# Moving one transposed piece of v from TensorE to the DMA, and the loads behind it to new places

## The chip, the cores and the metric

The kernel runs on one core of one Trainium2 chip. The metric is the device time of one execution in microseconds (us), median of several runs. The kernel before takes 569.44 us (three runs, 569.25 to 569.69). A profile's "span" is about 1.75 us shorter than the time of the same run (567.7 for a run of 569.45 us), so spans are compared with spans.

Engine names: PE is TensorE, DVE VectorE, ACT ScalarE, POOL GpSimd, SP SyncE; PEld is the weight load of TensorE. "L157" is line 157 of a kernel; the changed kernels have a few lines more or less, so the same statement can carry another number.

## The reference, cut to what matters

```python
# q, k, v: (4, 5824, 256)
qn = q / (norm(q, axis=1) + 1e-6);  kn = k / (norm(k, axis=1) + 1e-6)
a = softmax(kn.T @ qn / tau)                 # 256 x 256 for each batch
x = (v @ a).reshape(23296, 256)
out = (((x @ w1) * (x @ w2)) @ w3) @ w_out   # d_ff = 1024
```

The kernel folds `a` into w1 and w2 (a matrix Wf for each batch) and w3 into w_out (W_sb, once). For each chunk of 512 tokens there are then eight units of two products a and b from v transposed (each two matmuls of 512 columns), a multiply of the two, and output matmuls with W_sb.

## The kernel before

v arrives in six pieces of 8 x 128 tokens for each batch (the last is shorter); chunks 2p and 2p+1 use piece p. v has to be transposed, on PE (with a copy out of PSUM) or by a DMA transpose from SP:

```python
def transpose_half_on_pe(n, pi, h, on_act): ...      # 8 PE transposes, one copy on ACT or DVE
def transpose_piece(n, pi):
    ...
    nc.sync.dma_start_transpose(vT[:, pi * PIECE : (pi + 1) * PIECE, :, :], t[:, :, :])
```

All loads are issued by GpSimd, in program order, but for the first half pieces of q and k. Two kinds of tiny copies hold that queue back: `gate` reads the newest product (so the queue does not run ahead of PE), `hold` reads one element of a tile that a transpose writes (so the queue stands until the transpose has landed):

```python
def gate():                      # waits for the newest a*b tile
    nc.gpsimd.tensor_copy(gate_t, last_ab[0][:1, :1])
def hold(src):                   # waits for whatever writes src
    nc.gpsimd.tensor_copy(gate_t, src)
```

An agenda says at which place of PE's own order ("clock", in estimated us of PE work) each piece of side work is emitted, `at(place, cost, what)`. For batch 0:

```python
load_piece("v", 0, 1); load_piece("v", 0, 2)
nc.gpsimd.dma_start(out=wout_sb, ...); nc.gpsimd.dma_start(out=w3_bf, ...)     # right behind v
...
at(7.0, 0.5, lambda: transpose_half_on_pe(0, 1, 0, True))
at(8.0, 0.5, lambda: transpose_half_on_pe(0, 1, 1, False))
at(15.0, 0.0, transpose_w3)                       # four DMA transposes
at(15.0, 0.0, lambda: transpose_piece(0, 2))
for jt in range(FT):                              # w3 into w_out, 64 matmuls
    at(27.5 + 1.2 * jt, 0.87, lambda jt=jt: w_unit(jt))
moves = [("qk", 1, 0, 29.0), ("v", 0, 3, 30.0), ("v", 0, 4, 30.5), ("qk", 1, 1, 44.0), ...]
```

Output matmuls may start only when the eight w units are done; until then PE runs a and b units. The G matmuls (q and k of the next batch) are spread over the middle of each batch.

Of the kernel before, what the change touches and what calls it, by code (L numbers as in the profile page):

```python
# [15 lines left out]
P = 128  # L16
PIECE = 8
# [8 lines left out]
def kernel(  # L26
# [12 lines left out]
    nc = tc.nc  # L39
# [11 lines left out]
    FT = F // P  # L51
# [3 lines left out]
    NP_ = (NT + PIECE - 1) // PIECE  # L55
# [59 lines left out]
    def load_piece(nm, n, pi, cuts=()):  # L115

        new_piece(nm, n, pi)
        ends = [0, *cuts, LAST if pi == NP_ - 1 else PIECE]
        for lo, hi in zip(ends, ends[1:]):
            load_part(nm, n, pi, lo, hi)  # L120

    vTs = {}

    def new_vT(n):
        vTs[n] = (
            vT_pool.tile([P, NT - 1, CT, P], BF16, tag="vT", name=f"vT_{n}"),
            vT_pool.tile([P, CT, P + LEFT], BF16, tag="vTt", name=f"vTt_{n}"),
        )

    def pe_transpose(dst, src, tag, on_act):  # L130

        m = psum.tile([P, 8, P], BF16, tag=tag, name=f"tr_{nc.get_next_instruction_name()}", bufs={"ab": 4, "out": 3}[tag])
        for i, blk in enumerate(src):
            nc.tensor.transpose(m[:, i, :], blk, ident_b)
        if on_act:
            nc.scalar.copy(dst, m)
        else:
            nc.vector.tensor_copy(dst, m)

    def transpose_half_on_pe(n, pi, h, on_act):  # L140
        if pi == 0 and h == 0:
            new_vT(n)
        t = pieces["v", n, pi]
        i0 = 4 * h
        pe_transpose(
            vTs[n][0][:, pi * PIECE + i0 : pi * PIECE + i0 + 4, :, :].rearrange("p i c t -> p (i c) t"),
            [t[:, i0 + i, ct * P : (ct + 1) * P] for i in range(4) for ct in range(CT)],
            "out", on_act,
        )

    def transpose_piece(n, pi):
        if pi == 0:
            new_vT(n)
        vT, vTt = vTs[n]
        t = pieces.pop(("v", n, pi))
        if pi < NP_ - 1:
            nc.sync.dma_start_transpose(vT[:, pi * PIECE : (pi + 1) * PIECE, :, :], t[:, :, :])  # L157
        else:
            g = LAST - 1
            nc.sync.dma_start_transpose(vT[:, pi * PIECE : pi * PIECE + g, :, :], t[:, :g, :])  # L160

            first = n % 2 == 0
            nc.sync.dma_start_transpose(vTt[:, :, :P] if first else vTt[:, :, LEFT:], t[:, g, :])
            nc.sync.dma_start_transpose(vTt[:, :, P:] if first else vTt[:, :, :LEFT], t[:LEFT, g + 1, :])
# [52 lines left out]
    def squares(nm, pi, slots, end=False):  # L217

        if nm not in S:
            S[nm] = psum.tile([P, CT, P], F32, tag="out", name=f"sq{nm}_0", bufs=3)  # L220
        t = pieces[nm, 0, pi]
        for i in slots:
            for ct in range(CT):
                cs = slice(ct * P, (ct + 1) * P)
                nc.tensor.matmul(  # L225
                    S[nm][:, ct, :], lhsT=t[:, i, cs], rhs=t[:, i, cs],
                    start=(pi == 0 and i == 0 and ct == 0),
                    stop=(end and i == slots[-1] and ct == CT - 1), skip_group_check=True,
                )
# [211 lines left out]
    def at(t, cost, fn):  # L441
        seq[0] += 1
        agenda.append((t, seq[0], cost, fn))
# [22 lines left out]
    def hold(src):  # L466

        nc.gpsimd.tensor_copy(gate_t, src)  # L468
# [81 lines left out]
    def load_qk(n, pi):  # L550
        load_piece("q", n, pi)
        load_piece("k", n, pi)
# [13 lines left out]
    w3_bf = w3_wout[:, : FT * F].rearrange("p (j l) -> p j l", l=F)  # L566
    wout_sb = w3_wout[:, FT * F : FT * (F + D)].rearrange("p (l d) -> p l d", d=D)
    w3T = []
# [20 lines left out]
    w3r = moe_w3.rearrange("(jh jl) l -> jl jh l", jl=P)  # L589
# [29 lines left out]
    load_part("v", 0, 0, half, PIECE)  # L619
    load_piece("v", 0, 1)  # L620
    load_piece("v", 0, 2)
    nc.gpsimd.dma_start(out=wout_sb, in_=moe_w_out.rearrange("(lh ll) c -> ll lh c", ll=P))
    nc.gpsimd.dma_start(out=w3_bf, in_=w3r)
    squares("k", 4, whole)
    for sl in (lo, hi):
        squares("q", 4, sl)
# [19 lines left out]
    def w_unit(jt):  # L646
        m = psum.tile([P, 512], F32, tag="out", name=f"w_{jt}", bufs=3)
        for lt in range(FT):
            nc.tensor.matmul(  # L649
                m[:, :D], lhsT=w3T[jt // 2][:, jt % 2, lt, :], rhs=wout_sb[:, lt, :],  # L650
                start=(lt == 0), stop=(lt == FT - 1),
            )
        if jt % 2 == 0:
            nc.scalar.copy(W_sb[:, jt, :], m[:, :D])
        else:
            nc.vector.tensor_copy(W_sb[:, jt, :], m[:, :D])
        if jt == FT - 1:
            w_ready[0] = True

    def load_library():  # L660

        m = work.tile([P, 1], F32, tag="lib", name="lib", bufs=1)
        nc.gpsimd.partition_all_reduce(m, ones_f, P, ReduceOp.add)


    def make_agenda(b):
        agenda.clear()
        clock[0] = 0.0
        n = b + 1
        if b == 0:  # L670
            at(0.5, 0.87, soft0[5])
            for i in range(4):
                at((1.7, 2.6, 3.5, 3.9)[i], 0.43, soft0[7 + i])
            at(0.0, 0.0, load_library)
            at(4.6, 0.5, lambda: transpose_half_on_pe(0, 0, 1, False))
            at(7.0, 0.5, lambda: transpose_half_on_pe(0, 1, 0, True))
            at(8.0, 0.5, lambda: transpose_half_on_pe(0, 1, 1, False))
            at(15.0, 0.0, transpose_w3)
            at(15.0, 0.0, lambda: transpose_piece(0, 2))
            for jt in range(FT):  # L680
                at(27.5 + 1.2 * jt, 0.87, lambda jt=jt: w_unit(jt))
            moves = [("qk", 1, 0, 29.0), ("v", 0, 3, 30.0), ("v", 0, 4, 30.5), ("qk", 1, 1, 44.0), ("qk", 1, 2, 45.0)]
            moves += [("qk", 1, 3, 53.0), ("qk", 1, 4, 55.0), ("v", 0, 5, 61.0), ("qk", 1, 5, 73.0)]
            moves += [("v", 1, 0, 88.0), ("v", 1, 1, 98.0), ("v", 1, 2, 120.0), ("qk", 2, 0, 130.0)]
            t0, t1 = 54.0, 113.0
        else:
            moves = [("v", b, 3, 1.0), ("qk", n, 1, 10.0), ("qk", n, 2, 17.0), ("v", b, 4, 26.0), ("qk", n, 3, 38.0)]
            moves += [("v", b, 5, 46.0), ("qk", n, 4, 58.0), ("qk", n, 5, 66.0)]
            moves += [("v", n, 0, 76.0), ("v", n, 1, 86.0), ("v", n, 2, 96.0), ("qk", n + 1, 0, 108.0)]
            moves = [m for m in moves if m[1] < B]  # L690
            t0, t1 = 16.0, 98.0

        before = (0, 2) if b == 0 else None
        for nm, m, pi, t in moves:
            if before is not None and not (nm == "v" and before == (m, pi - 1) == (0, 3)):
                at(t, 0.0, lambda w=before: hold(vTs[w[0]][1][:1, 0, :1] if w[1] == NP_ - 1 else vTs[w[0]][0][:1, w[1] * PIECE, 0, :1]))
            at(t, 0.0, gate)
            if nm == "qk":
                at(t, 0.0, lambda m=m, pi=pi: load_qk(m, pi))
                before = None  # L700
            else:
                at(t, 0.0, lambda m=m, pi=pi: load_piece("v", m, pi))
                at(t + 4.0, 0.0, lambda m=m, pi=pi: transpose_piece(m, pi))
                before = (m, pi)
        if n == B:
            agenda.sort()
            return
        units = score_units(n)
        for i, (cst, fn) in enumerate(units):
            at(t0 + (t1 - t0) * i / len(units), cst, fn)  # L710
        soft = soft_units(n)
        for cst, t, fn in soft:
            at(t1 + 1.0 + t, cst, fn)
        agenda.sort()

    for b in range(B):
        make_agenda(b)
        for c in range(NCH):
            for j in range(FT):
                run_due()  # L720
                emit_ab(b, c, j)
                npop = 0
                lag = LAG
                if b == B - 1 and c >= NCH - 2:
                    lag = LAG_END if c == NCH - 1 else LAG + (LAG_END - LAG) * (j + 1) // FT
                while w_ready[0] and len(pend) > lag and npop < 2:
                    emit_out(*pend.pop(0))
                    npop += 1
                    run_due()
        run_due(1e9)  # L730
# [39 lines left out]
```

## Time and profile before

| | kernel before |
|---|---|
| time, median | 569.44 us |
| span | 567.7 us |
| PE busy | 557.6 us (98%) |
| chain that ended last | PE 93%, DMA 5% |
| first a matmul | 37.27 us |
| PE's last group of output matmuls starts | 562.19 us |
| from there to the end of the span | 5.51 us |

A line of a timeline: start and length in us, engine, line, operation, how many.

```profile
562.19 1.47 PE L521 MATMUL o<-W_sb,left 128*128 128x256 bf16 x12
```

### The profile page before, as it was taken

The numbers are of one execution on the slowest core, as the hardware profiler recorded it, in microseconds if no ns is written. First come the engines' busy times: TensorE is split into PE (matmuls) and PEld (weight loads), VectorE is DVE, ScalarE is ACT, GpSimd is POOL, SyncE is SP. The second block draws the span as 40 slices with busy tenths as digits, with TensorE's granted clock in tenths as the row PEclk, the third lists the DMA queues.
The fourth block names the chain that finished last, engine by engine and source line by source line (L and its number), as shares of the span: only waits on it lengthen the run. The fifth ranks groups of instructions, "written<-read, shape, count | busy, mean of one in ns | idle before, by whom it ended". The sixth has DMA issues, their size and how long they took to land.

```text
span 567.7 us, 10095 instructions
## 1 busy us (share of the span) xinstructions
PE 557.6 (98%) x3755; PEld 355.4 (63%) x3755; DVE 375.4 (66%) x581; ACT 338.7 (60%) x627; POOL 77.9 (14%) x163
## 2 busy tenths in 40 slices
PE   8799999999999999999999999999999999999997
PEld 5664566776656666666656566666655655665655
DVE  1047645888966577888766668787876665565564
ACT  1057536777766577777675567777765554454453
POOL 4260013120111111121210101030120000000000
PEclk9999999999999999999999999999999999999999
DMA  9999989978455796595661595765740325221011
GB/s 213 211 182 209 173 171 237 226 164 192 115 142 121 143 192 148 90 193 123 145 149 75 97 219 117 155 120 121 185 112 39 85 74 149 64 68 71 38 70 61
DMA packets 75104, 77.45 MB, mean 136 GB/s; under 512 B 54192, under 2 KB 58800, under 8 KB 75056
## 3 DMA queue, kind: packets, MB, share of 16 engines
q0 software_dynamic: 15760, 38.93, 39.3%
q1 hardware_dynamic: 59008, 37.23, 22.0%
q10 hardware_dynamic: 288, 0.66, 0.4%
q8 instruction: 29, 0.48, 0.3%
q14 instruction: 19, 0.16, 0.1%
HBM read 78.91 MB, written 23.86 MB: 181 GB/s over the span
## 4 chain that ended last, share of the span: by engine, by line
PE 93%; DMA 5%; ACT 1%; POOL 0%; issue 0%; DVE 0%; ACTq 0%; POOLq 0%
PE o L521 28%; PE b L476 28%; PE a L476 28%; PE G L192 5%; DMA k<-in_k_dram 5%; PE fold L363 2%; PE w L649 1%; ACT kr L283 0%; PE quarter L389 0%; POOL k L111 0%; POOL q L111 0%; PE sqk L225 0%; PE row L271 0%; ACT e L322 0%; ACT Wf L398 0%
## 5 line engine op out<-in xcount | busy, mean ns | idle before, releaser
L497 DVE TENSOR_TENSOR abs<-as,b 128x512 bf16<-128x512 bf16 x336 | 230.6, 687 | 143.9 <-ACT as L482 131.4
L482 ACT CAST as<-a 128x512 bf16<-128x512 f32 (+1 forms) x384 | 215.9, 562 | 170.4 <-DVE abs L497 84.7
L476 PEld LDWEIGHTS <-Wf 128*128 128x128 bf16 x1536 | 149.0, 98 | 102.3 <-ACT Wf L398 0.6
L476 PE MATMUL a<-vT,Wf 128*128 128x512 bf16 x704 | 209.6, 379 | 0.4 <-ACT Wf L398 0.4
L476 PE MATMUL b<-vT,Wf 128*128 128x512 bf16 x704 | 209.6, 379 | 0.0
L521 PE MATMUL o<-W_sb,abs 128*128 128x256 bf16 x1344 | 201.5, 273 | 0.0
L521 PEld LDWEIGHTS <-abs 128*128 128x128 bf16 x1344 | 131.2, 98 | 79.8 <-issue 0.2
L201 DVE TENSOR_TENSOR acc<-acc,sq 128x1024 f32<-128x1024 f32 x66 | 80.4, 1219 | 0.6 <-ACT sq L189 0.6
L192 PE MATMUL G<-k,q 128*128 128x256 bf16 x276 | 49.8, 273 | 0.0
L189 ACT ACTIVATE sq<-q 128x512 f32<-128x512 bf16 x66 | 41.8, 633 | 0.0
L189 ACT ACTIVATE sq<-k 128x512 f32<-128x512 bf16 x66 | 41.5, 629 | 0.0
L464 POOL COPY gate_t<-abs 1x1 bf16<-1x1 bf16 x39 | 10.5, 269 | 171.7 <-DVE abs L497 168.8
L543 DVE COPY osb<-o 128x512 f32<-128x512 f32 x44 | 30.1, 685 | 0.9 <-PE o L521 0.9
L192 PEld LDWEIGHTS <-q 128*128 128x128 bf16 x276 | 27.0, 98 | 3.1
L542 ACT COPY osb<-o 128x512 f32<-128x512 f32 x44 | 25.8, 586 | 4.1 <-PE o L521 2.1
L468 POOL COPY gate_t<-vT 1x1 bf16<-1x1 bf16 x16 | 3.1, 193 | 158.8 <-DMA vT<-v 158.8
L111 POOL DMA_DIRECT2D q<-in_q_dram x28 | 15.1, 540 | 12.5 <-DMA k<-in_k_dram 5.5
L370 ACT ACTIVATE Wf<-fold,rs 128x512 bf16<-128x512 f32 x15 | 10.3, 687 | 10.9 <-PE fold L363 8.7
L283 ACT ACTIVATE kr<-row 128x256 f32<-128x256 f32 x1 | 0.4, 383 | 26.1 <-PE row L271 26.1
L363 PE MATMUL fold<-w,e 128*128 128x512 bf16 x56 | 15.0, 379 | 0.0
L487 DVE TENSOR_TENSOR left<-as,b 128x192 bf16<-128x192 bf16 x32 | 11.3, 354 | 5.1 <-ACT as L482 2.7
L497 DVE TENSOR_TENSOR abq<-as,b 128x512 bf16<-128x512 bf16 x16 | 10.8, 686 | 5.0 <-ACT as L482 4.5
(98 smaller groups left out, 242.3 us busy)
## 6 DMA issues: line engine op xcount, KB each, us to landing
out_dram<-osb SPq DMA_DIRECT2D x44, 512.0 KB, 3.3
k<-in_k_dram POOLq DMA_DIRECT2D x19, 512.0 KB, 8.3
v<-in_v_dram POOLq DMA_DIRECT2D x19, 512.0 KB, 5.2
q<-in_q_dram POOLq DMA_DIRECT2D x18, 512.0 KB, 5.8
w_wout<-in_moe_w_dram POOLq DMA_DIRECT2D x1, 2048.0 KB, 22.7
k<-in_k_dram POOLq DMA_DIRECT2D x4, 320.0 KB, 8.8
v<-in_v_dram POOLq DMA_DIRECT2D x4, 320.0 KB, 4.9
q<-in_q_dram POOLq DMA_DIRECT2D x3, 320.0 KB, 4.1
```

The source lines that it names most:

```text
L111: nc.gpsimd.dma_start(out=pieces[nm, n, pi][:, lo:hi, :], in_=qk_main[nm, n][0][:, pi * PIECE + lo : pi * PIECE + hi, :])
L189: nc.scalar.activation(out=dst[:, :, part, :], in_=src[:, o : o + 2, :], func=AF.Square)
L192: nc.tensor.matmul(G[:, ct, :], lhsT=qt[:, i, ct * P : (ct + 1) * P], rhs=kt[:, i, :], start=(pr == 0 and part == 0 and ct == 0), stop=(pr ...
L201: nc.vector.tensor_add(accs[n], accs[n], sqs[0])
L363: nc.tensor.matmul(m, lhsT=st["e"][:, c2, c1 * P : (c1 + 1) * P], rhs=w12[:, c2, w, lo:hi], start=(c2 == 0), stop=(c2 == CT - 1),)
L476: nc.tensor.matmul(t[:, :n], lhsT=Wf[b][:, ct, w, j * P : (j + 1) * P], rhs=rhs_of(b, c, ct), start=(ct == 0), stop=(ct == CT - 1),)
L482: nc.scalar.copy(a_sb[:, :n], tiles[0][:, :n])
L487: nc.vector.tensor_mul(both, a_sb[:, :n], tiles[1][:, :n])
L497: nc.vector.tensor_mul(ab, a_sb, tiles[1])
L521: nc.tensor.matmul(tl[h][:, o, :], lhsT=lhsT, rhs=W_sb[:, j, :], start=(j == 0 and o == 0), stop=(j == FT - 1 and (small or o == 1)), skip ...
L542: nc.scalar.copy(o[:, 0:2, :], tl[0])
L543: nc.vector.tensor_copy(o[:, 2:4, :], tl[1])
```

## The change

The intent is to take eight plus eight PE transposes (v piece 1) out of PE's stream. In their place stands one DMA transpose. It is put ahead of the loads of w_out and w3, which are held until it has landed; the w units and the later loads move to fit, and v pieces 4 and 5 go behind more of the next batch's q and k. ("..." marks lines left out; the comment at the end was added for this text.)

```diff
-    nc.gpsimd.dma_start(out=wout_sb, ...)
-    nc.gpsimd.dma_start(out=w3_bf, in_=w3r)
...
-            at(7.0, 0.5, lambda: transpose_half_on_pe(0, 1, 0, True))
-            at(8.0, 0.5, lambda: transpose_half_on_pe(0, 1, 1, False))
-            at(15.0, 0.0, transpose_w3)
-            at(15.0, 0.0, lambda: transpose_piece(0, 2))
+            at(0.0, 0.0, lambda: transpose_piece(0, 2))
+            at(0.0, 0.0, lambda: transpose_piece(0, 1))
+            at(0.0, 0.0, lambda: hold(vTs[0][0][:1, PIECE, 0, :1]))
+            at(0.0, 0.0, load_w3)
+            at(16.0, 0.0, transpose_w3)
             for jt in range(FT):
-                at(27.5 + 1.2 * jt, 0.87, lambda jt=jt: w_unit(jt))
-            moves = [("qk", 1, 0, 29.0), ("v", 0, 3, 30.0), ("v", 0, 4, 30.5), ("qk", 1, 1, 44.0), ("qk", 1, 2, 45.0)]
-            moves += [("qk", 1, 3, 53.0), ("qk", 1, 4, 55.0), ("v", 0, 5, 61.0), ("qk", 1, 5, 73.0)]
-            moves += [("v", 1, 0, 88.0), ("v", 1, 1, 98.0), ...]
+                at(35.5 + 1.2 * jt, 0.87, lambda jt=jt: w_unit(jt))
+            moves = [("qk", 1, 0, 35.0), ("v", 0, 3, 35.5), ("qk", 1, 1, 49.0), ("qk", 1, 2, 51.0), ("qk", 1, 3, 55.0)]
+            moves += [("qk", 1, 4, 57.0), ("v", 0, 4, 60.0), ("qk", 1, 5, 80.0), ("v", 0, 5, 83.0)]
+            moves += [("v", 1, 0, 97.0), ("v", 1, 1, 106.0), ...]
...
-        before = (0, 2) if b == 0 else None
+        before = "w3" if b == 0 else None      # the first hold is now on the fourth w3 transpose
```

More of the change, by code (lines that the diff above doesn't have):

```diff
@@ L621 @@
     load_piece("v", 0, 2)
-    nc.gpsimd.dma_start(out=wout_sb, in_=moe_w_out.rearrange("(lh ll) c -> ll lh c", ll=P))
-    nc.gpsimd.dma_start(out=w3_bf, in_=w3r)
     squares("k", 4, whole)
@@ L658, in w_unit, with load_w3 @@
             w_ready[0] = True
+    def load_w3():
+        nc.gpsimd.dma_start(out=wout_sb, in_=moe_w_out.rearrange("(lh ll) c -> ll lh c", ll=P))
+        nc.gpsimd.dma_start(out=w3_bf, in_=w3r)
     def load_library():
@@ L675, in make_agenda @@
             at(4.6, 0.5, lambda: transpose_half_on_pe(0, 0, 1, False))
-            at(7.0, 0.5, lambda: transpose_half_on_pe(0, 1, 0, True))
-            at(8.0, 0.5, lambda: transpose_half_on_pe(0, 1, 1, False))
-            at(15.0, 0.0, transpose_w3)
-            at(15.0, 0.0, lambda: transpose_piece(0, 2))
+            at(0.0, 0.0, lambda: transpose_piece(0, 2))
[3 more added lines that the diff above has]
+            at(16.0, 0.0, transpose_w3)
             for jt in range(FT):
-                at(27.5 + 1.2 * jt, 0.87, lambda jt=jt: w_unit(jt))
-            moves = [("qk", 1, 0, 29.0), ("v", 0, 3, 30.0), ("v", 0, 4, 30.5), ("qk", 1, 1, 44.0), ("qk", 1, 2, 45.0)]
-            moves += [("qk", 1, 3, 53.0), ("qk", 1, 4, 55.0), ("v", 0, 5, 61.0), ("qk", 1, 5, 73.0)]
-            moves += [("v", 1, 0, 88.0), ("v", 1, 1, 98.0), ("v", 1, 2, 120.0), ("qk", 2, 0, 130.0)]
+                at(35.5 + 1.2 * jt, 0.87, lambda jt=jt: w_unit(jt))
+            moves = [("qk", 1, 0, 35.0), ("v", 0, 3, 35.5), ("qk", 1, 1, 49.0), ("qk", 1, 2, 51.0), ("qk", 1, 3, 55.0)]
+            moves += [("qk", 1, 4, 57.0), ("v", 0, 4, 60.0), ("qk", 1, 5, 80.0), ("v", 0, 5, 83.0)]
+            moves += [("v", 1, 0, 97.0), ("v", 1, 1, 106.0), ("v", 1, 2, 120.0), ("qk", 2, 0, 130.0)]
             t0, t1 = 54.0, 113.0
@@ L691, in make_agenda @@
             t0, t1 = 16.0, 98.0
-        before = (0, 2) if b == 0 else None
+        before = "w3" if b == 0 else None
         for nm, m, pi, t in moves:
             if before is not None and not (nm == "v" and before == (m, pi - 1) == (0, 3)):
-                at(t, 0.0, lambda w=before: hold(vTs[w[0]][1][:1, 0, :1] if w[1] == NP_ - 1 else vTs[w[0]][0][:1, w[1] * PIECE, 0, :1]))
+                at(t, 0.0, lambda w=before: hold(w3T[-1][:1, 1, FT - 1, :1] if w == "w3" else vTs[w[0]][1][:1, 0, :1] if w[1] == NP_ - 1 else vTs[w[0]][0][:1, w[1] * PIECE, 0, :1]))
             at(t, 0.0, gate)
```

## The prediction

> **What bounds the kernel now.** I read the page's busy shares and chain first, then the list of what PE waited for, then PE's timeline around the part that the change touches, then the timelines of the two engines that issue transfers.
>
> ```profile
> PE 557.6 (98%) x3755; PEld 355.4 (63%) x3755; DVE 375.4 (66%) x581; ACT 338.7 (60%) x627; POOL 77.9 (14%) x163
> ...
> PE 93%; DMA 5%; ACT 1%; POOL 0%; issue 0%; DVE 0%; ACTq 0%; POOLq 0%
> ```
>
> PE is busy for 557.6 of 567.7 us, and 93% of the chain that ended last is PE. The DMA share of the chain (5%) lies before 31 us, in the first loads of q and k, which the change leaves alone. The view of PE's waits says where PE idles:
>
> ```profile
> PE sqq L225 <- DMA q<-in_q_dram: 3.6, 3, 1.7
> PE warm_I-92_93 L213 <- DVE warm L78: 1.2, 1, 1.2
> PE a L476 <- ACT Wf L398: 0.4, 1, 0.4
> PE sum L340 <- ACT e L322: 0.4, 1, 0.4
> ```
>
> In the timeline all of these end by 37.27 us, when the first a matmul starts; after that no PE row carries an idle time. So from 37.27 us on the kernel is a dense, in-order stream of matmuls. Work taken out of it is worth its own length, but any operand that comes late is paid in full.
>
> **What the Trainium skill says.** Four places matter.
> - "TensorE: Matmul & The Clock Gate", Part 4: PE-mode transpose, gives about 275 ns for one 128x128 bf16 transpose in a kernel, with a copy out of PSUM to follow. The trace disagrees for a stream of them: eight start at 44.71 us and the next matmul starts at 45.16 us, so one costs 0.45/8 = 0.056 us of PE. I use the trace; with the page's figure I would expect five times the gain.
> - "DMA: Bandwidth & Descriptors", Anatomy of one DMA: a semaphore wait happens on the issuing sequencer, and the DMA engines just consume their queues. The trace agrees: the GpSimd queue stood at one hold for 34.8 us, and every load behind it in program order started later.
> - The same section fits 2.0 us + bytes/436e3 per load, 3.2 us for a 512 KB piece. The trace has 5.1 us for a piece on an empty queue (q at 73.73 us), so I use measured times.
> - The same page, DMA Transpose (X-bar): the plain transpose can be issued from Sync or Scalar only. The trace shows all of them on SP, one after the other.
>
> **The change part by part.** *Removed from PE:* the two half-piece transposes of v piece 1 (the order of PE's instructions has 16 matmuls and 16 weight loads fewer).
>
> ```profile
> 44.28 0.60 PE L476 MATMUL b<-vT,Wf 128*128 128x512 bf16 x2
> 44.71 0.61 PE L134 MATMUL tr_I-615_616<-ident_b,v 128*128 128x128 bf16 x8
> 45.16 0.60 PE L476 MATMUL a<-vT,Wf 128*128 128x512 bf16 x2
> 45.59 0.59 PE L476 MATMUL b<-vT,Wf 128*128 128x512 bf16 x2
> 46.02 0.61 PE L134 MATMUL tr_I-635_636<-ident_b,v 128*128 128x128 bf16 x8
> 46.47 0.38 PE L476 MATMUL a<-vT,Wf 128*128 128x512 bf16 x1
> ```
>
> From the starts: 45.16 - 44.71 = 0.45 us and 46.47 - 46.02 = 0.45 us, in all **0.90 us** on the path that sets the end. One 1.01 us copy on ACT and one 0.69 us copy on DVE go too; neither engine bounds this stage (a unit of a and b takes PE 0.863 us, against 0.56 us of cast on ACT and 0.69 us of multiply on DVE), so I count them as nothing.
>
> *Added:* one SP transpose of 512 KB for that piece, and a hold on GpSimd for it before w_out and w3 are loaded. This is all transfer work; the matmuls that remain are the same in number and kind. *Moved:* the w units, from place 27.5 to 35.5 of the kernel's own clock, and the loads of batch 1's q and k and of v pieces 3, 4 and 5.
>
> So the sum on PE is -0.90 us: 569.44 - 0.90 = **568.54 us** if no operand comes late. Whether one does is the real question, because the change makes a serial chain of transfers from v piece 2 to v piece 3, where before the w3 load overlapped everything. The rows that give the durations:
>
> ```profile
> 34.23 1.66 POOL L111 DMA_DIRECT2D v<-in_v_dram  x3
> 35.81 0.97 POOL L622 DMA_DIRECT2D w_wout<-in_moe_w_out_dram  x1
> 36.69 0.97 POOL L623 DMA_DIRECT2D w_wout<-in_moe_w_dram  x1
> ...
> 72.99 0.18 POOL L468 COPY gate_t<-vT 1x1 bf16<-1x1 bf16 x1 [34.80 <-DMA vT<-v]
> 73.23 0.18 POOL L464 COPY gate_t<-abs 1x1 bf16<-1x1 bf16 x1
> 73.73 0.60 POOL L111 DMA_DIRECT2D q<-in_q_dram  x1 [0.33 <-PE w L649]
> ```
>
> ```profile
> 59.49 9.41 SPq L574 DMA_TRANSPOSE w3T<-w_wout  x4
> 68.95 19.95 SPq L157 DMA_TRANSPOSE vT<-v  x3
> ```
>
> For the needs I laid the matmuls of the changed order end to end from 37.27 us, with the spacings of the trace (512 columns 0.216 us, 256 columns 0.108 us). The same sum for the kernel before puts the first w matmul at 65.34 us, where the trace has 65.59, so I add 0.25 us.
> 1. v piece 2 lands 11.6 us after its issue at 35.3: 46.9 us. The changed order transposes it first, piece 1 second. A transpose holds SP 1.6 us and lands some 4.3 us after issue when another is in flight: piece 1 is ready at 46.9 + 1.7 + 4.3 = 52.9. Chunk 2 needs it at 54.4. **Slack 1.5 us.**
> 2. Hold and w_out issue: w_out lands on an empty queue about 5.6 us later, at 58.5. w3 followed w_out by 9.9 us before (49.5 to 59.4), so it lands at 68.4. Its first transpose lands 4.3 us later, 72.7; the first w unit needs it at 73.3. **Slack 0.6 us.**
> 3. The fourth w3 transpose landed 11.9 us after w3 (59.4 to 71.3): 80.3 us. The last pair of w units needs it at 82.0. Slack 1.7 us.
> 4. The next loads hold for that fourth transpose: 0.7 us to the q issue (72.99 to 73.73), 10.1 us until the v piece behind q and k lands (73.73 to 83.8), 3.9 us for its transpose: 80.3 + 14.7 = 95.0. Chunk 6 needs v piece 3 at 94.8. **Slack -0.2 us**, where the kernel before had some 18 us (88 against 106). The w units now come later, so chunks 5 and 6 come earlier: PE has more a and b work to do before it may start the outputs.
> 5. Eight q and k pieces and v piece 4 (4.7 MB) and one output store (0.5 MB), at the 0.226 MB per us that 91.7 to 118.2 us showed for the same mix, from 95.7: 118.8, transposed 122.8. Chunk 8 needs it at 128.3. Slack 5 us.
> 6. v piece 5 lands about 136 and is transposed by 140; chunk 10 needs it at 159. GpSimd must also be free for batch 1's all-reduce at 153: behind v piece 5 it issues two more v pieces, and I make that about 151. Slack some 2 us.
>
> Steps 1 to 4 are one chain, so its lateness is paid once, at the worst of the four. My estimate for each slack is good to about 1.3 us, so the mean wait from step 4, with the others slightly better, is some 0.5 us, and no wait at all is about as likely as a wait. 568.54 + 0.4 gives **568.9 us**.
>
> **The rivals.** (A) *No late operand: the gain is the whole 0.90 us*, 568.5 us. For it: all places in the change are moved together, as by somebody who watched these slacks, and step 3's transposes no longer have v piece 2 behind them. (B) *A new PE wait takes the gain back or more*: 569.5 to 571 us, most likely at chunk 6 for v piece 3, else at the first w unit for w3T or at chunk 2. For it: slacks of 1.5, 0.6 and -0.2 us. Against it: each is the end of a chain of measured times, and one transfer faster by 1 us clears it. (C) *Softmax of batch 1 late through GpSimd*, which now carries v pieces 5, 1 and 2 in a different rhythm: the all-reduce starts late and PE waits up to 2 us at the column sums; 570 us. Before, e was ready about 1 us ahead of the sums, and GpSimd waited 12.8 us for DVE ahead of the all-reduce, so there is room. (D) *Nothing at all*, because transfers set the end: spoken against by a chain that is 93% PE.
>
> **Range and chances.** A gives the lower edge: 568.5 less the run-to-run spread of 0.2 to 0.3 us, 568.2. B or C with a wait of about 2 us gives the upper edge, 570.6. To get 2% (11.4 us) faster, the change would have to remove twelve times what it removes; to get 2% slower it needs a stall that lasts as long as several transfers, say a buffer that is held by a load which itself waits. I give 0.5% and 1%.
>
> **What would show each step right or wrong.** PE's busy time falls by about 0.9 us, with 16 transposes gone after 44 us. PE waits after 37.27 us: none (A), or one on DMA vT or w3T of under 2.5 us (B), or one at the sums on e (C). In GpSimd's timeline the hold ahead of w_out ends near 53 us and the one ahead of q near 80 us; in SP's timeline the w3 transposes start near 68.5 us and the transpose of v piece 3 near 91 us. The prediction is wrong if w3 starts or lands some microseconds off that, or if a wait shows up in a later batch, where I take all to be shifted but unchanged.

## The result, and the profile after

| | before | changed |
|---|---|---|
| time, median (6 runs each) | 569.41 us | 569.37 us |
| PE busy | 557.6 us | 555.9 us |
| PE's last group starts | 562.19 us | 562.02 us |
| from there to the end of the span | 5.51 us | 5.98 us |
| span of the profiled run | 567.7 us | 568.0 us |

The ratio of changed to before is 1.000, with a 95% interval of 0.9987 to 1.0013. A ratio is the mean time of one kernel's fast runs over that of the other's of the same rounds, so it is not quite the ratio of the medians quoted. The time is the same.

The 0.90 us did leave PE. First the page of the changed kernel:

```profile
PE 555.9 (98%) x3739; PEld 354.2 (62%) x3739; DVE 375.0 (66%) x580; ACT 338.5 (60%) x626; POOL 79.2 (14%) x165
```

3755 matmuls have become 3739, and one copy each has gone from DVE and ACT. PE's busy time fell by 1.7 us, not by the 0.9 expected, but only 0.87 us of that lies after 37 us (526.37 against 525.50); the rest is in the start, which the change leaves alone, and which differs between runs (in experiment 1 it is 2.4 us more busy than here). Next, what PE waited for (us in total, times, longest), in the changed kernel:

```profile
PE sqq L225 <- DMA q<-in_q_dram: 3.4, 3, 1.8
...
PE G L192 <- DMA k<-in_k_dram: 0.8, 1, 0.8
```

The second line is new: a G matmul of batch 1 waits for a piece of k. PE's timeline shows when:

```profile
101.82 0.60 PE L521 MATMUL o<-W_sb,abs 128*128 128x256 bf16 x4
103.18 0.38 PE L192 MATMUL G<-k,q 128*128 128x256 bf16 x2 [0.75 <-DMA k<-in_k_dram]
103.39 0.60 PE L521 MATMUL o<-W_sb,abs 128*128 128x256 bf16 x4
```

Now GpSimd's timeline of the changed kernel, to answer the rows of before in the prediction:

```profile
53.02 0.18 POOL L468 COPY gate_t<-vT 1x1 bf16<-1x1 bf16 x1 [16.65 <-DMA vT<-v]
53.25 0.95 POOL L659 DMA_DIRECT2D w_wout<-in_moe_w_out_dram  x1
...
79.07 0.18 POOL L468 COPY gate_t<-w3T 1x1 bf16<-1x1 bf16 x1 [23.99 <-DMA w3T<-w_wout]
...
94.63 0.18 POOL L468 COPY gate_t<-vT 1x1 bf16<-1x1 bf16 x1 [13.09 <-DMA vT<-v]
94.87 0.18 POOL L464 COPY gate_t<-abs 1x1 bf16<-1x1 bf16 x1
95.36 0.53 POOL L111 DMA_DIRECT2D q<-in_q_dram  x1 [0.31 <-PE a L476]
95.88 0.54 POOL L111 DMA_DIRECT2D k<-in_k_dram  x1
```

and SP's:

```profile
47.25 3.65 SPq L157 DMA_TRANSPOSE vT<-v  x2
69.22 7.73 SPq L574 DMA_TRANSPOSE w3T<-w_wout  x4
90.82 1.58 SPq L157 DMA_TRANSPOSE vT<-v  x1
```

Three holds in a row (53.0, 79.1, 94.6 us) make one serial chain: v piece 1, then w3 and its transposes, then q, k and v piece 3, and only then k piece 1, issued at 95.88 us. That transfer took 7.3 us to land, at 103.2 us, and PE's G matmul starts at 103.18. In the kernel before the same piece was issued at 92.22 us and PE needed it at about 101.5 us.

The last group of the changed kernel:

```profile
562.02 1.47 PE L521 MATMUL o<-W_sb,left 128*128 128x256 bf16 x12
```

From the first a matmul (37.27 before, 37.21 changed) to the start of the last group it is 524.92 us before and 524.81 changed. The sum of the two terms, -0.90 + 0.75 = -0.15 us, is close to this difference of -0.11 us. But the span grew by 0.3 us, so something after PE's last group (two copies, three small stores, and SP's final waits) has to account for some 0.45 us. (These are single profiled runs. The medians differ by 0.04 us only, so the 0.3 us is not to be read as a loss.) SP's final waits in the last microseconds differ; before:

```profile
SPq L765 <- DMA out_dram<-oleft: 0.8, 1, 0.8
SPq L765 <- PEq L765: 0.7, 2, 0.5
SPq L765 <- DMA out_dram<-osb: 0.3, 1, 0.3
```

and changed:

```profile
SPq L768 <- DMA out_dram<-oleft: 1.6, 1, 1.6
SPq L768 <- PEq L768: 0.7, 2, 0.5
```

The stores themselves land equally fast (2.3 and 2.5 us after issue in both), but SP's last wait is on another of them.

### The profile page after: what moved, and what is told of

It is laid out like the page before. It is cut to its first block, busy times and chain, and to the rows that moved or that the text cites. A ratio compares the mean times of both kernels' runs of the same rounds, so it can differ in the third digit from the quotient of the medians.

```text
span 568.0 us, 10068 instructions
## 1 busy us (share of the span) xinstructions
PE 555.9 (98%) x3739; PEld 354.2 (62%) x3739; DVE 375.0 (66%) x580; ACT 338.5 (60%) x626; POOL 79.2 (14%) x165
## 4 chain that ended last, share of the span: by engine, by line
PE 92%; DMA 6%; ACT 1%; POOL 0%; issue 0%; DVE 0%; ACTq 0%; POOLq 0%
PE o L521 28%; PE a L476 27%; PE b L476 27%; DMA k<-in_k_dram 6%; PE G L192 5%; PE fold L363 2%; PE w L647 1%; ACT kr L283 0%; POOL q L111 0%; PE quarter L389 0%; POOL k L111 0%; PE sqk L225 0%; PE row L271 0%; ACT e L322 0%; ACT Wf L398 0%
## 5 line engine op out<-in xcount | busy, mean ns | idle before, releaser
L468 POOL COPY gate_t<-vT 1x1 bf16<-1x1 bf16 x17 | 4.7, 277 | 171.9 <-DMA vT<-v 171.9
L111 POOL DMA_DIRECT2D v<-in_v_dram x25 | 13.5, 544 | 4.4 <-issue 3.2
```

The lines of the kernel that those rows point to most:

```text
L111: nc.gpsimd.dma_start(out=pieces[nm, n, pi][:, lo:hi, :], in_=qk_main[nm, n][0][:, pi * PIECE + lo : pi * PIECE + hi, :])
```

## The experiments

There were two questions: does the new wait for k account for what PE lost, and what is the longer tail? There was also a third, what each moved part is for.

**Experiment 1, e1_k_later: the G matmuls a little later.** From k piece 1 on, G units get later places, so that the piece is there.

```diff
-            at(t0 + (t1 - t0) * i / len(units), cst, fn)
+            late = 1.7 * (len(units) - i) / (len(units) - 12) if b == 0 and i >= 12 else 0.0
+            at(t0 + (t1 - t0) * i / len(units) + late, cst, fn)
```

> The changed kernel with batch 1's G matmuls from k piece 1 on placed up to 1.7 us later in PE's order; nothing else differs. Theory: the change does save 0.90 us of PE, and gives 0.75 us of it back in one place, the wait of G for k piece 1 at 103.18 us (that piece landed at 103.2 us, 7.3 us after its issue at 95.88). With G at 103.9 us the piece is there: no PE wait after 37.3 us, the last group of output matmuls starts some 0.75 us earlier than in the changed kernel (562.02), near 561.2, and the time is 568.6 us (ratio to the kernel before 0.9986). Rival: the gain was never there, since something else sets the end: the wait goes but the last output matmuls still start near 562.0 and the time stays at 569.4.

Measured: 568.89 us (568.64 to 569.12, five runs), against 569.28 us for the kernel before in the same rounds, ratio 0.999 (0.9977 to 1.0002). The interval of the times just includes no change, so the trace has to decide, and it does: PE waits for nothing after 37.11 us, and the last group starts where the theory put it.

```profile
561.25 1.47 PE L521 MATMUL o<-W_sb,left 128*128 128x256 bf16 x12
```

That is 0.94 us earlier than before. The time fell by only about 0.4, because the tail is again long: 567.2 - 561.25 = 5.95 us.

**Experiment 2, e2_pe_again: the 16 PE transposes back.** On top of experiment 1, v piece 1 is transposed on PE again and the hold is set on v piece 2; all else stays.

```diff
-            at(0.0, 0.0, lambda: transpose_piece(0, 1))
-            at(0.0, 0.0, lambda: hold(vTs[0][0][:1, PIECE, 0, :1]))
+            at(7.0, 0.5, lambda: transpose_half_on_pe(0, 1, 0, True))
+            at(8.0, 0.5, lambda: transpose_half_on_pe(0, 1, 1, False))
+            at(0.0, 0.0, lambda: hold(vTs[0][0][:1, 2 * PIECE, 0, :1]))
```

> e1_k_later with v piece 1 put back on PE (16 transposes) and the hold ahead of w_out and w3 set on v piece 2 instead. Measures the removed cost by itself, beside e1_k_later of the same rounds. Theory: 0.90 us more than e1_k_later, so about 569.5 us, no PE wait after 37.3 us, w3 starts some 2 us earlier. Rival, the Trainium skill's 275 ns for one transpose: 16 of them would be 4.4 us more. Second rival, PE transposes hide in slack: no difference to e1_k_later.

Measured: the last group starts at 562.17 us, 0.92 us after that of experiment 1 (the first a starts within 0.1 us in both: 37.02 and 37.11), and PE has no new wait on a transfer. It does have one of 0.2 us on DVE late in the program, and from the first a to the last group it takes 525.15 us against 524.14. So the 16 transposes cost 0.8 to 0.9 us of PE by themselves, about as predicted, neither nothing nor 4.4 us (16 times the 275 ns that the prediction quotes). (w3 is issued about 3 us earlier than in the changed kernel, not 2: the hold ends at 49.89 us.) The tail is short again, 5.43 us. The median, 569.89 us (569.42 to 571.36), is 1.0 us above experiment 1; its spread is too wide to say more than the trace does.

**Experiment 3, e4_v4_early: v piece 4 back to its old place.**

```diff
-            moves = [..., ("v", 0, 3, 35.5), ("qk", 1, 1, 49.0), ..., ("v", 0, 4, 60.0), ...]
+            moves = [..., ("v", 0, 3, 35.5), ("v", 0, 4, 36.0), ("qk", 1, 1, 49.0), ...]
```

> The changed kernel with only the place of v piece 4 undone: it is loaded right behind v piece 3, as before, ahead of batch 1's q and k pieces 1 to 4. Theory: the transfers form one serial chain that is now tied to PE, so one more piece in it (2.5 us of load, then its transpose) comes late in full: the hold ahead of q piece 1 ends near 97 to 98 us instead of 94.6, k piece 1 lands near 106, G waits 3 to 4 us there instead of 0.75, and the time is 571.5 to 572.5 us. Rival: the order of the loads does not matter because there is slack behind: within 0.5 us of the changed kernel.

Measured: 575.23 us (570.79 to 576.30, four runs), ratio 1.0086 to the kernel before. The hold ends at 96.33 us and G waits 3.9 us, as expected; the time is 3 us worse than expected. PE's timeline of the profiled run (574.41 us) shows part of why:

```profile
101.78 0.60 PE L521 MATMUL o<-W_sb,abs 128*128 128x256 bf16 x4
106.28 0.59 PE L192 MATMUL G<-k,q 128*128 128x256 bf16 x2 [3.90 <-DMA k<-in_k_dram]
106.66 1.06 PE L521 MATMUL o<-W_sb,abs 128*128 128x256 bf16 x4
107.52 0.63 PE L192 MATMUL G<-k,q 128*128 128x256 bf16 x2
107.94 1.06 PE L476 MATMUL a<-vT,Wf 128*128 128x512 bf16 x2
...
109.60 0.60 PE L521 MATMUL o<-W_sb,abs 128*128 128x256 bf16 x4
```

After the wait, four output matmuls take 0.86 us from start to start (106.66 to 107.52) where 0.43 is usual. The view of stretches says that the granted clock was 0.53 from 106 to 108 us and 0.62 from 108 to 110 us, then 1.00 again (the third number from the right is the clock):

```profile
106.00:108.00 2.00, 1.72 (x9) 1.22 (x9) 0.00 (x0) 0.63 (x1) 0.00 (x0) 0.53 1.06 272
108.00:110.00 2.00, 2.00 (x9) 0.91 (x8) 0.13 (x1) 0.96 (x2) 0.00 (x0) 0.62 1.10 223
```

The Trainium skill, "TensorE: Matmul & The Clock Gate", Part 1, says that PE falls to half its clock after an idle window of about 3.4 us and needs about as long a busy one to come back. The trace agrees: after 0.75 us of idleness the clock stayed at 1.00, after 3.9 us it halved for some 3 us. Here the last group starts at 566.71 us, 4.7 us later than in the changed kernel: 3.15 us more waiting and about 1.5 us at half clock. The spread of the four runs fits this: the one of 570.79 us has a mean clock of 0.999, the slower three have 0.993 to 0.996. Only one of them was traced in this detail, so that the fast one escaped the half clock is not shown.

**Experiment 4, e5_no_hold: w_out and w3 load beside the transposes.**

```diff
-            at(0.0, 0.0, lambda: hold(vTs[0][0][:1, PIECE, 0, :1]))
```

> The changed kernel without the hold ahead of w_out and w3, so that their loads run beside the two transposes of v pieces 2 and 1, which still go first on SP. Theory: a transpose beside a load lands a few us later but not more, v piece 1 is there by 53 us (needed at 54.2), w3 lands 3 to 5 us earlier than in the changed kernel, all that follows moves up by as much, the wait for k piece 1 is gone, and the time is 568.6 us. Rival, the reason for which the hold may have been put in: the transposes queue behind the packets of w3 and land 8 us or more after issue, PE waits at chunk 2 (54.2 us) for v piece 1, and the time is 570 to 573 us.

Measured: 580.93 us (579.26 to 581.46), ratio 1.0196 (1.0182 to 1.0211). My theory fell, and the rival was right in kind but too mild. SP's timeline, then PE's:

```profile
46.98 14.88 SPq L157 DMA_TRANSPOSE vT<-v  x2
```

```profile
64.00 1.03 PE L476 MATMUL a<-vT,Wf 128*128 128x512 bf16 x2 [9.68 <-DMA vT<-v]
64.83 1.06 PE L476 MATMUL b<-vT,Wf 128*128 128x512 bf16 x2
```

Two transposes hold SP for 14.88 us, where they took 3.65 us with nothing beside them. PE waits 9.68 us for v piece 1 and then runs at half clock for some 4.3 us (the products are 0.85 us apart until 68.24, and the clock from 64 to 68 us is 0.50). The DMA view explains the size: alone (47.2 to 53.0 us of the changed kernel) the two transposes are 4160 packets of 1.05 MB, about 250 bytes each, moved at up to 297 GB/s. Beside w3 (48 to 62 us here) 2683 such packets got through while 1200 load packets carried 2.16 MB, about 1.8 KB each. The Trainium skill, "DMA: Bandwidth & Descriptors", Queues, rings and completion order, says that each DMA engine takes turns between the queues that have work, a packet at a time. That fits: small packets that take turns with packets seven times their size get little of the bytes. Whether a packet of the profile is what the page calls a packet isn't shown, so that the turns are the cause is argued from these counts; that the transposes slow down fourfold is shown.

**Experiment 5, e3_alone: the DMA transpose alone.** In the kernel before, v piece 1 goes to a DMA transpose; no hold, no other move.

```diff
-            at(7.0, 0.5, lambda: transpose_half_on_pe(0, 1, 0, True))
-            at(8.0, 0.5, lambda: transpose_half_on_pe(0, 1, 1, False))
+            at(0.0, 0.0, lambda: transpose_piece(0, 1))
```

> The kernel before with only v piece 1 taken from PE to a DMA transpose, at once when it lands; the hold, the places of w3 and of the other loads stay as before. After e5_no_hold (two transposes beside the loads of w_out and w3 took 15 us of SP, PE waited 9.7 us) I expect: the transpose starts near 44.5 us, lands 8 to 15 us later, PE waits at chunk 2 (54.2 us) for 0 to 6 us, and the time is 570 to 576 us. Rival, the hold and the new places are not needed: no wait and 568.5 us.

Measured: 580.72 us (one run, so its state is unknown, but far outside any spread). I had expected at most 576. One transpose holds SP for 13.11 us, and PE waits 9.0 us:

```profile
45.76 13.11 SPq L157 DMA_TRANSPOSE vT<-v  x1
```

So the hold and the new places are not tuning around the idea; without them it costs 11 us. (Its tail is 5.97 us; it too has one SP transfer more than the kernel before.)

**Experiment 6, e6_tail, and experiment 7, e7_before_split: the tail.** Four kernels with one SP transfer more than before had a tail of 5.9 to 6.0 us. Experiment 6 takes one transfer away from SP in the kernel of experiment 1, experiment 7 adds one to the kernel before.

```diff
# experiment 6
-                nc.sync.dma_start(out=rows[:, 4 * c : 4 * c + 4, :], in_=o)
+                (nc.gpsimd if b == B - 1 and c == 6 else nc.sync).dma_start(out=rows[:, 4 * c : 4 * c + 4, :], in_=o)
# experiment 7, for b == B - 1 and c == 6
+                nc.sync.dma_start(out=rows[:, 4 * c : 4 * c + 2, :], in_=o[:, 0:2, :])
+                nc.sync.dma_start(out=rows[:, 4 * c + 2 : 4 * c + 4, :], in_=o[:, 2:4, :])
```

> e1_k_later with one of the output stores of the last batch (chunk 6) issued by GpSimd instead of SP, so that the number of transfers issued by SP and ACT is again that of the kernel before. From the start of PE's last group of output matmuls to the end of the span it took 5.51 us in the kernel before and 5.43 in e2_pe_again, but 5.98, 5.95, 5.89 and 5.91 in the four kernels with one more SP transfer (changed, e1, e4, e5), though the last transfers take equally long to land. Theory: the eight completion semaphores are handed out in turn, and one transfer more moves the last store to another of them, which SP's final waits reach in another order: 0.45 us. Then the tail is 5.4 to 5.5 us here, PE's last group starts at 561.2 as in e1, and the time is 568.4 us. Rival: the tail is longer for another reason (chance, or how full the queues are): it stays at 5.9 and the time at 568.9.

> The kernel before with one store of the last batch (chunk 6) split in two, so one more SP transfer and nothing else. Theory of the semaphores' turn: PE's last group starts at 562.2 as before, the tail grows from 5.51 to 5.9 to 6.0 us, the time is 0.4 to 0.5 us above the kernel before of the same rounds. Rival: no change.

Measured: experiment 6 takes **568.55 us** (568.32 to 568.66) against 569.46 us before, ratio 0.998 (0.9968 to 0.9993): clear of noise, and the best version. Its last group starts at 561.04 us and its tail is 5.46 us. SP's final waits have their old form:

```profile
SPq L769 <- DMA out_dram<-oleft: 0.8, 1, 0.8
SPq L769 <- PEq L769: 0.7, 2, 0.5
SPq L769 <- DMA out_dram<-osb: 0.3, 1, 0.3
```

Experiment 7 takes 570.03 us (569.68 to 570.84), ratio 1.0011 (0.9997 to 1.0025), which includes no change, so here the trace decides. Its last group starts at 561.97 us and its tail is 5.93 us, with the one wait of 1.6 us. So one transfer more or less on SP moves the tail by 0.4 to 0.5 us in either direction, whether it is a transpose of batch 0 or a store of the last batch. What differs can be read in the compiled programs (built again from the kernels; this is no view of the profile). SP and ACT together issue 88 transfers in the kernels with a short tail and 89 in the others, and these take eight completion semaphores in turn. The last store of SP signals semaphore 7 where the tail is short and semaphore 0 where it is long, and SP's closing list checks the eight in the order 0 to 7. Where the tail is long, SP thus waits for the last store first and has seven checks left when it has landed. That these checks take the 0.4 to 0.5 us is argued: no view times them. If it is so, what counts is the turn, and one more transfer need not lengthen another program.

**Control, after_again.** The changed kernel unaltered, in the rounds of experiments 6 and 7.

> The changed kernel unaltered, to compare with e6_tail and the kernel before on one chip in the same rounds. Theory: 569.2 to 569.5 us, 0.2 us or less off the kernel before: PE's last group at 562.0, wait for k piece 1 of 0.6 to 0.9 us, tail 5.9 us. Rival, chip-to-chip differences hid a gain of 0.9 us: 568.5 us.

Measured: 569.58 us (568.75 to 570.15), ratio 1.000 (0.9987 to 1.0012), G waits 0.72 us, last group at 561.89, tail 5.9 us. The account repeats.

## Why the prediction was right or wrong

The time, 569.37 us, lies in the range, 0.5 us above the point. The steps:

- **The sum on PE (-0.90 us): right.** Experiment 2 measured 0.8 to 0.9 us. The trace's spacing of 0.056 us for a transpose in a stream held. The 275 ns of the Trainium skill ("TensorE: Matmul & The Clock Gate", Part 4) is a duration, so the prediction was wrong to say that the trace disagrees: one transpose lasts 219 ns in this trace, but in a stream the next starts 0.056 us later, and it is the spacing that the sum needs.
- **Steps 1 to 4, the serial chain: right in shape and within 1.3 us in each place.** v piece 1 was there at 53.0 us (52.9 predicted), w3's transposes began at 69.2 (68.4) and ended at 79.1 (80.3), v piece 3 was transposed at 94.6 (95.0). The slacks were as thin as said: the first w matmul starts at 73.14 us, just as its transpose lands (69.22 + 3.9 = 73.1), and chunk 6 starts at 94.66, just behind v piece 3. None of these places shows a wait of a matmul (a weight load before the first w matmul waited 0.3 us). That is close to luck: at chunk 6 the hold for the same piece ends 0.03 us before the matmul starts.
- **Step 5: mis-sized.** v piece 4 was transposed at 127.5 us, not 122.8. The 0.226 MB per us is too high even for the stretch that it was read from: the DMA view gives 5.6 MB from 91.7 to 118.2 us before, 0.21 MB per us, and 5.3 MB from 95.4 to 122.8 us changed, 0.19. Chunk 8, which the wait for k had moved back too, started at 129.25 us and did not wait.
- **Step 6: right.** The all-reduce waited 0.4 us for DVE and none for its place in GpSimd's queue; rival C did not happen.
- **What the list of needs left out.** I followed the chain to v pieces 3, 4 and 5 but did not check k piece 1, which is next in the same queue. The same arithmetic gives it: issued 1.3 us after the hold, 7 us to land, about 103 us, against a G matmul due at about 102.3. Rival B named the mechanism, a late operand paid in full, and put it at chunk 6, at the first w unit or at chunk 2. It happened at G, with 0.75 us. (That is PE's idle time in the profile. From start to start, 101.82 to 103.18 less the usual 0.43, it is 0.93; from the first a to the last group the kernels with the wait take 524.8 us, those of experiments 1 and 6 without it 524.1 and 523.9. So its size is good to 0.2 us.)
- **"All to be shifted but unchanged" afterwards: wrong, by 0.45 us.** The tail after PE's last group grew, which nothing in my working looked at.

So the point estimate of a 0.5 us gain was made from +0.4 us for waits (the prediction works out 0.5 and then adds 0.4); the two terms that came were +0.75 (wait for k, shown by experiment 1) and +0.45 (tail, shown by experiments 6 and 7). Together they exceed the 0.90, and 0.3 us is by how much the profiled span grew. The range held because it left room for one late operand of up to 2 us; that the tail, which the working did not look at, fitted into the same room was luck.

## What to carry to other kernels

When one engine runs dense and in order, list every operand behind each hold, not only those of the stream that you moved; here the next piece in the queue was the late one. A DMA transpose beside a large load is slow enough to decide a schedule (one held SP for 13.11 us here, two alone for 3.65), so give it a stretch of its own. And before a gain below one microsecond is judged, split the span at the last work of the bounding engine: the end of the program can move by half a microsecond because one transfer more was issued long before, as here.

## What the Trainium skill lacked or had wrong

- "TensorE: Matmul & The Clock Gate", Part 4: it gives 275 ns for a PE transpose in a kernel and does not say that a stream of them costs far less. Here one lasts 219 ns but the next starts 0.056 us later (16 for 0.90 us).
- "DMA: Bandwidth & Descriptors", DMA Transpose (X-bar): it says nothing of what a transpose costs beside ordinary loads. Two of 512 KB held SP for 3.65 us alone and for 14.88 us beside the load of w3.
- "DMA: Bandwidth & Descriptors", Anatomy of one DMA: the fit gives 3.2 us for the 512 KB that a piece has in SBUF (4.4 us, an estimate by the same fit, for the 1 MB of f32 that is read); 5.1 us were measured for a v piece with next to no other transfer in flight (issued at 153.70 us in the changed kernel). The load also converts f32 to bf16; whether that is the reason isn't shown.
- No page that I read has it: with 89 transfers from SP and ACT instead of 88 the time after PE's last group was about 5.95 us instead of about 5.45.
